# Float64 weights to float32: two ScalarE passes and one VectorE instruction per chunk in place of one and three

## The chip, the core and the metric

The kernel runs on one core of a Trainium2 chip. The metric is the device time of one execution in microseconds, taken as the median of three runs. Five engines work side by side, each through its own list of instructions in order: TensorE (PE: matmuls, with its weight loads listed as PEld), VectorE (DVE), ScalarE (ACT), GpSimd (POOL) and SyncE (SP), which here only issues DMA transfers. An instruction at the head of a list that waits for another engine or for a transfer holds up everything behind it in that list.

## What is computed

Eight batches of 576 tokens go through a two-step attention with 8 heads and 32 packed queries, then through a Fourier mixing, a normalisation and a two-layer network with residual:

```python
p_packed = sm_attn(p, k, v)              # p: 32 packed queries per head
out = sm_attn(q, p_packed, p_packed)
x = out.transpose(0, 2, 1, 3).reshape(B, S, H * D)
...
mixed = np.real(np.fft.fft(np.fft.fft(x, axis=1), axis=2)).astype(np.float32)
u = x + mixed
un = (u - mean(u)) / np.sqrt(var(u) + 1e-06)
ch = np.maximum(un @ w_ch1, 0.0) @ w_ch2
return (u + ch).astype(np.float32)
```

`w_ch1` (512 x 2048) and `w_ch2` (2048 x 512) arrive as float64; every other input is float32.

## The kernel before

**Tiles.** The 4608 token rows are worked in 9 tiles of 512 rows. `front(b)` computes attention and Fourier mixing of batch b, which fill the rows `u`; `ffn` runs the network on one tile. While `ffn` of tile t runs on PE, `front(t + 1)` is issued in small steps in between, so that the two share all engines. Before tile 0 stands only `front(0)`.

**The network.** The hidden dimension is cut into 16 blocks j (`NJ`). Per block, `up` (L637) makes 12 matmuls of 128x512 into a bank `ph`; ACT takes the relu of it, rounded to a matmul's precision, as `hh` (L643), DVE the remainder as `hl` (L644); then `down` (L654) makes 12 matmuls with the `hh` and `hl` of the block before into `acc`. So each block has one `hl`, and the 16 `hl` of a tile are a clock of its progress; I count them from hl 0. Each weight block is split likewise: `wr_h` by ACT (L99) and `wr_l` by POOL (L100).

**The weights.** There are 32 chunks of 128x512 numbers: `w1f[:, j]` and `w2f[:, j]` for each j. The float64 chunk is loaded as pairs of 32-bit words (low, high), 512 KB, into a staging place: the first six into parts of `w1f` and `w2f` that are still free, the others in turn into one place in `ubuf` and two buffers `wst`. `load_weights` (L167 to L170) turns it into float32 bits in place of the final chunk `c`: ACT takes the absolute value of the high word, read as a float32, times 2^-112 (which moves the exponent's bias); DVE shifts it left by 3, then ors in the three top bits of the low word, then the sign bit of the high word. The chunks are converted once, during `front(0)` and tile 0 (`LEAD` = 2 blocks ahead in the code); all other tiles find them in place.

**What sets the order.** From tile 1 on the order on PE, DVE, ACT and POOL is that of the code (`manual_schedule`, L738). Up to the end of tile 0 a scheduler of the framework orders each engine's list by its own estimate of the times, so a change in `load_weights` moves everything around it. The loads of keys (`kp`), values (`vt`) and queries (`qt`) for `front(1)` share one pool of two buffers (`ld`, L222) and stand in SP's list between the weight loads (L155). Such a load waits until the matmuls that read the buffer's last content are done; a weight load waits until DVE has finished with its staging place.

Of the kernel before, what the change touches and what calls it, by code (L numbers as in the profile page):

```python
# [9 lines left out]
F32 = mybir.dt.float32  # L10
F32R = mybir.dt.float32r
I32 = mybir.dt.int32
AF = mybir.ActivationFunctionType
ALU = mybir.AluOpType
AX = mybir.AxisListType
# [36 lines left out]
NE = 289  # L52
N2 = 258
REBIAS = 2.0 ** -112

# [20 lines left out]
def tile_kernel(ctx, tc, kpT, qT, v, w1, w2, tabs, tabR, tabB, tabT, sel, ident_d, out):  # L78
    nc = tc.nc
# [32 lines left out]

    nc.scalar.activation(small.tile([P, 1], F32, tag="ri", name="warm"), mhalf, AF.Exp)
    ubuf = cpool.tile([P, NU, DM], F32, name="ubuf")
# [26 lines left out]
    def spot(n, part, shape):  # L141

        t = (w1f, w2f)[n].rearrange("p j n -> p (j n)")[:, (part % NJ) * DM:]
        size = shape[1] * shape[2]
        return t[:, 0:size].rearrange("p (a n) -> p a n", a=shape[1])

    def fetch(j, n):
        i = stages.pop(0)
        if i is None:
            st = work.tile([P, 512, 2], I32, tag="wst", name="wst", bufs=2)  # L150
        elif i < 0:
            st = spot(n, i, [P, 512, 2]).bitcast(I32)
        else:
            st = ubuf[:, i:i + 2, :].rearrange("p a n -> p (a n)").bitcast(I32).rearrange("p (n t) -> p n t", t=2)
        nc.sync.dma_start(st, (w1, w2)[n][:, j, :].bitcast(I32).rearrange("p (n t) -> p n t", t=2))  # L155
        fetched[j, n] = st

    def load_weights(j):

        for n, dst in enumerate((w1f, w2f)):  # L160
            if (j, n) not in fetched:
                fetch(j, n)
            st = fetched.pop((j, n))
            low, high = st[:, :, 0], st[:, :, 1]
            c = dst[:, j, :].bitcast(I32)

            nc.scalar.activation(c.bitcast(F32), high.bitcast(F32), AF.Abs, scale=REBIAS)  # L167
            nc.vector.tensor_scalar(c, c, 3, None, ALU.logical_shift_left)
            nc.vector.scalar_tensor_tensor(c, low, 29, c, ALU.logical_shift_right, ALU.bitwise_or)  # L169
            nc.vector.scalar_tensor_tensor(c, high, -0x80000000, c,  # L170
                                           ALU.bitwise_and, ALU.bitwise_or)

# [26 lines left out]
    def statistics(key):  # L201
# [3 lines left out]
        def squares():  # L205
            junk = work.tile([P, DM], F32, tag="tmp", name="junk", bufs=3)
            nc.scalar.activation(junk, u, AF.Square, bias=st[:, 1:2], scale=-1.0, accum_out=st[:, 2:3])  # L207

# [22 lines left out]
    def front(b):  # L231
# [31 lines left out]
        def scores(*gs):  # L263
# [11 lines left out]
            for g in gs:  # L275
# [7 lines left out]
                for c, w in ((1, slice(512, S)), (0, slice(0, 512))):  # L283
                    nc.scalar.activation(e1[:, w], sc[g][c], AF.Exp,
                                         bias=nb, scale=0.125, accum_out=sm2[:, c:c + 1])
# [80 lines left out]
        def less_one(g):  # L366
# [6 lines left out]
            def exps():  # L373
                nc.scalar.activation(s2, s2, AF.Exp, scale=0.125)
                nc.scalar.activation(s2, s2, AF.Copy, bias=-1.0)

# [338 lines left out]
    for j in range(ORDER[0].count("D"), LEAD):  # L715
        load_weights(j)
# [3 lines left out]
    for t, (first, tk) in enumerate(tiles):  # L720

        gen = front(t + 1) if t + 1 < B else iter(())
        ended = []

        def step(i):

            next_step()
            if t > 0 and i in (0, 2):
                next(rest, None)
            elif not ended and next(gen, None) == "rest":  # L730
                ended.append(gen)
            if t == 0 and i % 2 == 0 and i // 2 + LEAD < NJ:
                load_weights(i // 2 + LEAD)
            assert i < 2 * NJ - 1 or t + 1 >= B or ended

        nxt = Turned(tiles[t + 1][1]) if t + 1 < len(tiles) else None

        with tc.manual_schedule(engines=MANUAL) if t > 0 else nullcontext():  # L738
            ffn(first, cur, step, nxt, t + 1 >= B)
        cur, rest = nxt, gen  # L740
# [112 lines left out]
```

## Time and profile before

| what | us |
|---|---|
| median of 3 runs (1038.54 to 1040.67) | 1039.46 |
| span of the profiled execution, first to last instruction | 1035.7 |
| the part of the median outside such a span | 3.8 |
| hl 0 of tile 0 starts at | 70.18 |
| hl 0 of tile 1 starts at | 201.82 |
| hl 0 of tile 2 starts at | 310.76 |

The page gives the profiled execution its span alone (its own device time is not listed), so I set the 3.8 us between span and median down as a constant. The first 70 us are `front(0)`; tile 0 takes 131.6 us from its hl 0 to the next tile's, tile 1 takes 108.9. In the views, busy times are per engine, "x" counts instructions, and the row of a wait gives the total, the number of times and the longest.

### The profile page before, as it was taken

The numbers are of one execution on the slowest core, as the hardware profiler recorded it, in microseconds if no ns is written. First come the engines' busy times: TensorE is split into PE (matmuls) and PEld (weight loads), VectorE is DVE, ScalarE is ACT, GpSimd is POOL, SyncE is SP. The second block draws the span as 40 slices with busy tenths as digits, with TensorE's granted clock in tenths as the row PEclk, the third lists the DMA queues.
The fourth block names the chain that finished last, engine by engine and source line by source line (L and its number), as shares of the span: only waits on it lengthen the run. The fifth ranks groups of instructions, "written<-read, shape, count | busy, mean of one in ns | idle before, by whom it ended". The sixth has DMA issues, their size and how long they took to land.

```text
span 1035.7 us, 14903 instructions
## 1 busy us (share of the span) xinstructions
PE 975.5 (94%) x5692; PEld 796.0 (77%) x5692; DVE 631.8 (61%) x1291; ACT 423.7 (41%) x878; POOL 472.2 (46%) x426
## 2 busy tenths in 40 slices
PE   4298789999999999999999999999999999999998
PEld 2276567878887888878877887788778888887886
DVE  4889999468565775578555946685658562114112
ACT  3445445334444444444354344444444443333322
POOL 3625545355344543454335434543345444444443
PEclk9599989999999999999999999999999999999999
DMA  9227424130003100310022002200120000001001
GB/s 359 96 67 231 132 63 122 63 123 1 1 23 118 47 1 1 138 49 1 1 95 92 1 1 92 95 1 1 47 92 0 2 11 31 0 1 41 1 1 41
DMA packets 18184, 59.10 MB, mean 57 GB/s; under 512 B 2166, under 2 KB 3008, under 8 KB 18112
## 3 DMA queue, kind: packets, MB, share of 16 engines
q1 hardware_dynamic: 17136, 56.70, 16.0%
q0 software_dynamic: 976, 1.44, 0.5%
q8 instruction: 45, 0.74, 0.3%
q14 instruction: 27, 0.22, 0.1%
HBM read 48.70 MB, written 9.44 MB: 56 GB/s over the span
## 4 chain that ended last, share of the span: by engine, by line
PE 75%; DVE 15%; ACT 4%; DMA 3%; issue 2%; POOL 1%; SPq 0%; ACTq 0%; DVEq 0%; POOLq 0%
PE ph L637 34%; PE acc L654 30%; DVE ubuf L557 2%; DVE turned L409 1%; DMA w2f<-w 1%; ACT hh L643 1%; DVE w2f L169 1%; ACT junk L207 1%; PE po L316 1%; DVE turned L405 1%; DMA w2f<-v 1%; DVE hl L644 1%; DVE w1f L169 1%; PE untp L598 1%; POOL wr_l L100 1%
## 5 line engine op out<-in xcount | busy, mean ns | idle before, releaser
L100 POOL TENSOR_TENSOR wr_l<-w1f,wr_h 128x512 fp32r<-128x512 f32 x144 | 191.0, 1326 | 397.5 <-ACT wr_h L99 397.3
L644 DVE SCALAR_TENSOR_TENSOR hl<-ph,hh 128x512 fp32r<-128x512 f32 x144 | 98.7, 686 | 300.8 <-ACT hh L643 300.5
L637 PE MATMUL ph<-uh,wr_h 128*128 128x512 f32 (+1 forms) x580 | 231.3, 399 | 12.4 <-DVE hl L644 10.4
L100 POOL TENSOR_TENSOR wr_l<-w2f,wr_h 128x512 fp32r<-128x512 f32 x144 | 193.7, 1345 | 96.2 <-ACT wr_h L99 89.2
L654 PE MATMUL acc<-wr_l,hh 128*128 128x512 f32 x576 | 227.7, 395 | 2.9 <-POOL wr_l L100 2.9
L637 PE MATMUL ph<-uh,wr_l 128*128 128x512 f32 (+1 forms) x580 | 228.7, 394 | 0.0
L637 PE MATMUL ph<-ul,wr_h 128*128 128x512 f32 (+1 forms) x580 | 228.5, 394 | 0.0
L654 PE MATMUL acc<-wr_h,hh 128*128 128x512 f32 x576 | 228.3, 396 | 0.1
L654 PE MATMUL acc<-wr_h,hl 128*128 128x512 f32 x576 | 226.3, 393 | 0.0
L643 ACT ACTIVATE hh<-ph 128x512 fp32r<-128x512 f32 x144 | 85.9, 596 | 282.9 <-PE ph L637 282.6
L637 PEld LDWEIGHTS ph<-uh,wr_h 128*128 128x128 f32 x580 | 109.5, 189 | 47.1 <-DVE hl L644 13.0
L654 PEld LDWEIGHTS acc<-wr_l,hh 128*128 128x128 f32 x576 | 108.5, 188 | 26.6 <-POOL wr_l L100 5.3
L637 PEld LDWEIGHTS ph<-uh,wr_l 128*128 128x128 f32 x580 | 109.6, 189 | 24.0
L654 PEld LDWEIGHTS acc<-wr_h,hh 128*128 128x128 f32 x576 | 108.6, 189 | 24.8 <-ACT hh L643 1.0
L637 PEld LDWEIGHTS ph<-ul,wr_h 128*128 128x128 f32 x580 | 109.8, 189 | 21.8
L654 PEld LDWEIGHTS acc<-wr_h,hl 128*128 128x128 f32 x576 | 108.4, 188 | 23.1
L99 ACT CAST wr_h<-w2f 128x512 fp32r<-128x512 f32 x144 | 89.4, 621 | 10.4 <-PE ph L637 8.8
L99 ACT CAST wr_h<-w1f 128x512 fp32r<-128x512 f32 x144 | 88.4, 614 | 10.4 <-PE ph L637 3.1
L207 ACT ACTIVATE junk<-ubuf,stat 128x512 f32<-128x512 f32 x36 | 25.8, 717 | 71.1 <-DVE stat L203 71.1
L227 PE MATMUL py<-gh,fh 128*128 128x258 f32 x64 | 19.6, 307 | 28.6 <-ACT fh L469 28.6
L598 PE MATMUL untp<-ident,un 128*128 128x128 f32 x144 | 38.2, 282 | 2.4 <-DVE stat L203 2.0
L227 PEld LDWEIGHTS py<-gh,fh 128*128 128x128 f32 x64 | 13.1, 204 | 30.1 <-ACT fh L469 29.6
(201 smaller groups left out, 1349.0 us busy)
## 6 DMA issues: line engine op xcount, KB each, us to landing
kp<-kpT SPq DMA_DIRECT2D x16, 608.0 KB, 4.9
out<-ubuf SPq DMA_DIRECT2D x36, 256.0 KB, 2.1
vt<-v SPq DMA_DIRECT2D x14, 640.0 KB, 4.9
wst<-w SPq DMA_DIRECT2D x17, 512.0 KB, 3.7
qt<-qT SPq DMA_DIRECT2D x14, 576.0 KB, 4.9
ubuf<-w SPq DMA_DIRECT2D x9, 512.0 KB, 3.7
w1f<-w SPq DMA_DIRECT2D x3, 512.0 KB, 13.5
w2f<-w SPq DMA_DIRECT2D x3, 512.0 KB, 12.5
```

Of the source, the lines that this page charges most:

```text
L99: nc.scalar.copy(hi, src)
L100: (lo_eng or nc.vector).tensor_tensor(lo, src, hi.bitcast(F32), ALU.subtract)
L169: nc.vector.scalar_tensor_tensor(c, low, 29, c, ALU.logical_shift_right, ALU.bitwise_or)
L207: nc.scalar.activation(junk, u, AF.Square, bias=st[:, 1:2], scale=-1.0, accum_out=st[:, 2:3])
L227: nc.tensor.matmul(o, lh, rh, start=first, stop=False)
L316: nc.tensor.matmul(po[h * NPK:(h + 1) * NPK, :D], e1T[g][:kk, c, h * NPK:(h + 1) * NPK], vt[:kk, c, h * D:(h + 1) * D], start=(c == 0), st ...
L557: nc.vector.scalar_tensor_tensor(u_of[key], qe, sign, pe, ALU.mult, ALU.add, accum_out=stat_of[key][:, 0:1])
L598: nc.tensor.transpose(tp[:, c * P:(c + 1) * P], un[:, c * P:(c + 1) * P], ident)
L637: nc.tensor.matmul(ph[:, t], l[:, c * P:(c + 1) * P], r[:, c, t], start=(k == 0), stop=(k == 11))
L643: nc.scalar.activation(hh[:, :T], ph[:, :T], AF.Relu)
L644: nc.vector.scalar_tensor_tensor(hl[:, :T], ph[:, :T], 0.0, hh[:, :T].bitcast(F32), ALU.max, ALU.subtract)
L654: nc.tensor.matmul(acc[i], l[:, w], r, start=(j == 0 and k == 0), stop=(j == NJ - 1 and k == 2))
```

## The change

Per chunk, ACT now makes two passes and DVE one instruction:

```diff
+U8 = mybir.dt.uint8
...
+SIGN = -2.0 ** 32
...
-            low, high = st[:, :, 0], st[:, :, 1]
+            high = st[:, :, 1]
+            fifth = st.rearrange("p n t -> p (n t)").bitcast(U8).rearrange("p (n t) -> p n t", t=8)[:, :, 3]
             c = dst[:, j, :].bitcast(I32)
 
-            nc.scalar.activation(c.bitcast(F32), high.bitcast(F32), AF.Abs, scale=REBIAS)
-            nc.vector.tensor_scalar(c, c, 3, None, ALU.logical_shift_left)
-            nc.vector.scalar_tensor_tensor(c, low, 29, c, ALU.logical_shift_right, ALU.bitwise_or)
-            nc.vector.scalar_tensor_tensor(c, high, -0x80000000, c,
-                                           ALU.bitwise_and, ALU.bitwise_or)
+            nc.scalar.activation(c.bitcast(F32), high.bitcast(F32), AF.Prelu, scale=REBIAS, alpha=SIGN)
+            nc.scalar.activation(high, fifth, AF.Copy, scale=1.0 / 32, bias=-31.0 / 64)
+            nc.vector.scalar_tensor_tensor(c, c, 3, high, ALU.logical_shift_left, ALU.bitwise_or)
```

The first pass is a parametric relu: a positive number is scaled by 2^-112 as before; a negative one is multiplied by -2^32 as well, which makes it positive and sets a bit of the exponent that the shift by 3 carries into the sign's place. The second pass reads one byte of each 8, the low word's top byte, divides by 32 with an offset that makes the rounding a floor, and writes the result, the three top bits, as an integer over the high word. DVE then shifts and ors in one instruction. The DVE instruction now reads the staging place only after both passes, and a second ACT pass stands in ACT's list for each chunk.

The scheduler's lists move. First ACT's list in tile 0 as it was, from behind hh 3 up to hh 4 (`w1f`, `w2f` are chunks, `wst` and `ubuf` staging places, `pph` and `bdh` are of front(1)):

```order
L167 ACTIVATE w2f<-wst 128x512
L167 ACTIVATE w1f<-wst 128x512
L99 CAST wr_h<-w1f 128x512
L344 CAST pph<-pptp 128x128
L167 ACTIVATE w2f<-ubuf 128x512
L99 CAST bdh<-bd 128x256
L99 CAST wr_h<-w2f 128x512
L643 ACTIVATE hh<-ph 128x512
```

The same place now, from behind hh 3 up to hh 4 (line numbers are those of the changed kernel: L170 and L171 are the two passes, L101 is the cast, L644 is hh):

```order
L170 ACTIVATE w2f<-ubuf 128x512
L171 ACTIVATE ubuf<-ubuf 128x512
L170 ACTIVATE w1f<-wst 128x512
L101 CAST wr_h<-w1f 128x512
L171 ACTIVATE wst<-wst 128x512
L345 CAST pph<-pptp 128x128
L170 ACTIVATE w2f<-wst 128x512
L171 ACTIVATE wst<-wst 128x512
L101 CAST bdh<-bd 128x256
L170 ACTIVATE w1f<-ubuf 128x512
L644 ACTIVATE hh<-ph 128x512
```

Four chunks stand ahead of this hh where three stood, each with one pass more. Over the whole list, 15 chunks have passed ACT ahead of hh 0 where 9 had, and all 32 ahead of hh 7 where 22 had.

Next DVE in tile 0, from hl 2 to hl 3 (`pp` is of front(1)), before:

```order
L644 SCALAR_TENSOR_TENSOR hl<-ph,hh 128x512
L321 TENSOR_SCALAR pp_864<-po,ri 128x128
L168 TENSOR_SCALAR w1f<-w1f 128x512
L169 SCALAR_TENSOR_TENSOR w1f<-wst,w1f 128x512
L168 TENSOR_SCALAR w2f<-w2f 128x512
L170 SCALAR_TENSOR_TENSOR w1f<-wst,w1f 128x512
L169 SCALAR_TENSOR_TENSOR w2f<-wst,w2f 128x512
L170 SCALAR_TENSOR_TENSOR w2f<-wst,w2f 128x512
L168 TENSOR_SCALAR w1f<-w1f 128x512
L169 SCALAR_TENSOR_TENSOR w1f<-ubuf,w1f 128x512
L170 SCALAR_TENSOR_TENSOR w1f<-ubuf,w1f 128x512
L644 SCALAR_TENSOR_TENSOR hl<-ph,hh 128x512
```

And now, from hl 2 to hl 3 (L172 is the one instruction that is left per chunk, L645 is hl):

```order
L645 SCALAR_TENSOR_TENSOR hl<-ph,hh 128x512
L322 TENSOR_SCALAR pp_856<-po,ri 128x128
L172 SCALAR_TENSOR_TENSOR w1f<-w1f,ubuf 128x512
L172 SCALAR_TENSOR_TENSOR w2f<-w2f,wst 128x512
L172 SCALAR_TENSOR_TENSOR w1f<-w1f,wst 128x512
L645 SCALAR_TENSOR_TENSOR hl<-ph,hh 128x512
```

Nine conversion instructions between two hl became three; again three chunks.

Last SP's list, from the first staged chunk to the loads of the values, as a piece before:

```order
L155 DMA ubuf<-w 128x1024
L155 DMA wst<-w 128x1024 x2
L223 DMA vt<-v 128x1280
L155 DMA ubuf<-w 128x1024
L223 DMA vt<-v 128x1280
L155 DMA wst<-w 128x1024 x2
```

and now:

```order
L157 DMA ubuf<-w 128x1024
L157 DMA wst<-w 128x1024 x2
L157 DMA ubuf<-w 128x1024
L157 DMA wst<-w 128x1024 x2
L157 DMA ubuf<-w 128x1024
L157 DMA wst<-w 128x1024 x2
L224 DMA vt<-v 128x1280
L157 DMA ubuf<-w 128x1024
L157 DMA wst<-w 128x1024
L224 DMA vt<-v 128x1280
```

Six more weight loads stand ahead of the first load of values, and two in place of one between the two.

## The prediction

> **What bounds the kernel now.** I began with the page: which engine is busy in which slice of 26 us.
>
> ```profile
> span 1035.7 us, 14903 instructions
> ...
> DVE  4889999468565775578555946685658562114112
> ```
>
> DVE's row reads 9 from the fourth to the seventh slice and falls to 4 in the eighth: from about 78 to 180 us, tile 0, it is full, and nowhere later. So I took the pace of tile 0 from the timeline of DVE, by the starts of hl, one per block:
>
> ```profile
> 70.18 0.69 DVE L644 SCALAR_TENSOR_TENSOR hl<-ph,hh 128x512 fp32r<-128x512 f32 x1 [0.22 <-ACT hh L643]
> 129.46 0.68 DVE L644 SCALAR_TENSOR_TENSOR hl<-ph,hh 128x512 fp32r<-128x512 f32 x1
> 201.82 0.69 DVE L644 SCALAR_TENSOR_TENSOR hl<-ph,hh 128x512 fp32r<-128x512 f32 x1 [1.89 <-ACT hh L643]
> 247.26 0.65 DVE L644 SCALAR_TENSOR_TENSOR hl<-ph,hh 128x512 fp32r<-128x512 f32 x1
> 310.76 0.69 DVE L644 SCALAR_TENSOR_TENSOR hl<-ph,hh 128x512 fp32r<-128x512 f32 x1 [1.26 <-ACT hh L643]
> ```
>
> The rows are hl 0 and hl 7 of tile 0, hl 0 and hl 7 of tile 1, hl 0 of tile 2. From hl 0 to hl 7 tile 0 takes 59.3 us where tile 1 takes 45.4; from hl 7 to the next hl 0 it takes 72.4 where tile 1 takes 63.5. Tile 1 does the same work without conversions, and the last work of its front besides. So tile 0 is 13.9 + 8.9 = 22.8 us over a tile that PE alone paces. The busy times by stretch agree:
>
> ```profile
> core 0: us, PE busy (x) PEld busy (x) DVE busy (x) ACT busy (x) POOL busy (x), PEclk, DMA share, GB/s
> 70.20:129.50 59.30, 50.04 (x308) 36.21 (x308) 57.66 (x91) 27.01 (x54) 31.34 (x23) 0.97 0.60 188
> 129.50:201.80 72.30, 65.72 (x315) 54.23 (x316) 57.86 (x124) 31.85 (x65) 32.43 (x27) 0.95 0.26 81
> 201.80:310.80 109.00, 108.19 (x663) 88.99 (x662) 71.86 (x153) 47.18 (x101) 50.13 (x43) 1.00 0.12 41
> ```
>
> In the first half of tile 0 DVE works 57.7 of 59.3 us, while PE idles 9.3 and ACT over half the time; in tile 1 PE is full at clock 1.00. PE's waits from 66 to 190 us name the holder:
>
> ```profile
> PE ph L637 <- DVE hl L644: 10.4, 6, 3.7
> PE py L227 <- ACT fh L469: 3.4, 1, 3.4
> ```
>
> It is hl, which DVE does late; and each gap costs clock behind it (0.97 and 0.95). From tile 1 on the lists are those of the code, unchanged, so **only the time up to 201.8 us can change.**
>
> **What is removed on DVE.** The conversions of the three lines (L168, L169, L170, two rows each: first and second half of tile 0):
>
> ```profile
> 70.20:129.50 59.30, 9.73 (x15) 0.97 0.60 188
> 129.50:181.00 51.50, 4.35 (x11) 0.93 0.32 93
> ...
> 70.20:129.50 59.30, 16.51 (x15) 0.97 0.60 188
> 129.50:181.00 51.50, 8.02 (x11) 0.93 0.32 93
> ...
> 70.20:129.50 59.30, 11.01 (x14) 0.97 0.60 188
> 129.50:181.00 51.50, 12.09 (x12) 0.93 0.32 93
> ```
>
> That is 37.3 us in the first half and 24.5 in the second; without them 20.4 and 33.4 of other DVE work stay. By the new order 15 chunks are done ahead of hl 0, the other 17 between hl 0 and hl 7, none later. What one instruction costs, from the answers on lines L169 and L167 (min/median/max in ns):
>
> ```profile
> L169 DVE SCALAR_TENSOR_TENSOR w1f<-wst,w1f x8: 676/838/1672, 77.9 to 169.2; 128x512 int32<-128x512 int32 x8
> L167 ACT ACTIVATE w2f<-wst x9: 659/672/677, 34.1 to 174.7; 128x512 f32<-128x512 f32 x9
> ```
>
> The new DVE instruction has L169's form and operands, so 0.68 to 1.67 us each; I take 0.84, the median: 17 x 0.84 = 14.3 us (11.6 to 28). DVE then has 34.7 us of work in the first half, and is no longer the bound.
>
> The spread has a known shape. The Trainium skill (SBUF — State Buffer, section "Who interferes with whom") says that a DVE instruction with two SBUF inputs contends with a GpSimd instruction that reads SBUF, the later one blocked to the other's end, and that ACT never waits for anyone. The trace agrees: L169 reaches 1672 ns, ACT's pass stays within 659 to 677. By that rule the instruction that is kept is of the kind that still waits, and the sum would take 28 us for the 17 if each met one; it would leave DVE under 50 us, below the half.
>
> **What is added on ACT.** In the first half ACT's conversions take:
>
> ```profile
> 70.20:129.50 59.30, 8.86 (x14) 0.97 0.60 188
> ```
>
> Its other work there is 27.0 - 8.9 = 18.2 us. After: 17 chunks x 2 passes x 0.67 = 22.8 us, so 41 us in all; it fits. The trace has no parametric relu, no pass that reads single bytes 8 apart, and none that writes 32-bit words 8 bytes apart. Its read counterpart, the 8-byte-strided L167, is the nearest row (0.67); the upper end is 1.67, the worst L169. I take 0.67, the row that it is nearest to. Faster passes would gain nothing further, since ACT isn't the bound.
>
> **What paces the first half then: PE or the supply of chunks.** PE alone needs tile 1's 45.4 us. The supply is this: SP's waits up to 182 us, and the stretch without transfers ahead of tile 0:
>
> ```profile
> SPq L155 <- DVE w1f L170: 58.3, 12, 15.2
> SPq L223 <- PE s L259: 44.6, 2, 44.0
> SPq L155 <- DVE w2f L170: 30.1, 11, 5.1
> ...
> 40.00:70.00 30.00, 23.30 (x160) 21.20 (x160) 24.18 (x61) 14.48 (x33) 10.94 (x26) 0.75 0.00 1
> ```
>
> SP stood 44 us behind the first load of values, which waits for the score matmuls of front(1); all weight loads waited behind it, and 88 us went by waiting for DVE to free staging places. In the new list six more weight loads come ahead of that load, into those empty 30 us. What is left for the first half, by the list of transfers (KB each, us to landing) and the rate from 70 to 110 us:
>
> ```profile
> kp<-kpT SPq DMA_DIRECT2D x16, 608.0 KB, 4.9
> vt<-v SPq DMA_DIRECT2D x14, 640.0 KB, 4.9
> wst<-w SPq DMA_DIRECT2D x17, 512.0 KB, 3.7
> qt<-qT SPq DMA_DIRECT2D x14, 576.0 KB, 4.9
> ...
> 70.00:110.00 40.00, 36.58 (x246) 26.83 (x242) 38.18 (x62) 19.54 (x41) 20.35 (x15) 0.96 0.71 223
> ```
>
> 17 weight chunks, 2 vt, 2 qt and 1 kp are 12.0 MB. At 223 GB/s that is 54 us; but DMA was only 0.71 busy then, and 0.71 of 54, 38 us, is the other end. With three staging places a turn is 3.7 (landing) + 1.3 (two passes) + 0.84 + about 1.5 in queues = 7.3 us, so 17 chunks take 17 x 7.3 / 3 = 41 us, plus the five other loads in the same queue, 3.0 MB, 13 us at that rate if nothing overlaps. **I take 50.8 us for hl 0 to hl 7**, between 46.5 (PE) and 55 (supply), nearer to the middle than to either: a gain of 8.5 us (4.3 to 12.8).
>
> **The second half.** No chunk is left for it; 33.4 us of DVE work stand in some 65. The bound is PE's 63.5 us, a gain of 8.9. Of the waits, the 3.4 us for fh stay possible, since they end a chain of small DVE, POOL and ACT steps on the weights of front(1), which the scheduler has moved together. I take 66.9 us, **a gain of 5.5** (1 to 9).
>
> **The start of tile 0.** Ahead of hl 0 DVE does 15 conversion instructions for 19 shorter and longer ones: about even. ACT does 30 passes there for 9; three chunks' passes now stand between the last spectra and the last uh cast, which lets PE start:
>
> ```profile
> 65.72 0.58 ACT L99 CAST uh<-untp 128x512 fp32r<-128x512 f32 x1 [1.02 <-PE untp L598]
> ```
>
> The cover is ACT's idle time (it was idle over half of 40 to 70 us: 14.5 of 30 busy). Without it the cost is six passes, 4 us; with all of it and a freer DVE, -1. I take a **loss of 0.5**.
>
> **Sum:** -8.5 - 5.5 + 0.5 = -13.5 us on the span of 1035.7, so 1022.2; with the 3.8 us between span and median, 1026.0.
>
> **Rivals.**
> 1. *PE paces all of tile 0.* Chunks come early enough and the chain of front(1) keeps up: 12.8 + 8.9 - 0.5 = 21.2, so 1018.3. For it: 30 us of empty DMA time are put to use. Against it: 54 us of transfers at the rate seen.
> 2. *The supply stays the bound.* hl 7 stays near 129, the second half alone gains: 5.5 - 0.5, so 1034.5. For it: ACT already waits for chunks (below).
> 3. *A loop through the lists, and slower.* A chunk's load waits for DVE's instruction behind one hl, and its first pass stands ahead of the next hh but one or the next:
>
> ```profile
> ACT w2f L167 <- DMA wst<-w: 9.4, 6, 3.7
> ...
> L643 ACT ACTIVATE hh<-ph 128x512 fp32r<-128x512 f32 x144 | 85.9, 596 | 282.9 <-PE ph L637 282.6
> ```
>
> Here are ACT's wait for such loads and hh's duration (596 ns). A wait that used to cost ACT only idle time would then hold hh, hl, and through hl the next load. One turn is hl 0.69 + the instruction 0.84 + landing 3.7 + pass 0.67 + hh 0.60: 6.5 us; with both passes of two further chunks, 4 x 0.67, and a landing of 4.9 as for values, it is 10.4. It decides from 8.5 us a block on (59.3 / 7). At 10.4 in all seven: 73 us, 13.5 lost, 0.5 at the start, 5.5 regained: 1048. Against it: in the new list only hh 2 and hh 4 stand behind a chunk whose load follows the hl just before; the others have a block more.
> 4. *ACT's passes are dear.* At 1.3 us each ACT needs 18.2 + 44 = 62 us in the first half and becomes its bound: 3 to 5 us lost there, 5.5 regained: about 1039.
> 5. *The change brings more than it says: table loads.*
>
> ```profile
> 0.73 1.28 ACT L113 ACT_TABLE_LOAD   x1 [0.73 <-PEq L845]
> ```
>
> If the parametric relu didn't share a table with exp, each turn between the two in ACT's list (8) would cost such a load: 10 us at 1.28, all of it if on the path, so 1036. The new list still has one such load in all. The Trainium skill (ScalarE: Activation LUTs, section "Table sets: the hidden batching unit") names relu and abs, not this function, as members of exp's set, and puts a switch at about 2.7 us; by it the time would be some 21 us longer, about 1047. No run here shows a second load.
>
> **How the numbers follow.** Chances: forecast (1021 to 1031.5) 0.57, rival 1 0.14, rival 2 0.15, rival 3 0.07, rival 4 0.04, rival 5 0.03. The range runs from 1017 to 1035, which takes in the forecast and the first two rivals; the three bad ends of the sum at once (4.3, 1 and a late start by 4) would give 1038, the three good ones 1017. This kernel's measurement tells 0.2%, 2 us, from no change: faster (under 1037.4) is the forecast, rivals 1 and 2 and part of the others, 0.87; within it 0.04; slower 0.09.
>
> **What would show it.** DVE's row falls to 5 or 6 in the slices from 78 to 180 us; hl 7 of tile 0 starts near 121 and hl 0 of tile 1 near 188; PE's wait for hl falls under 4 us; weight transfers appear between 45 and 65 us; the ACT passes read 0.67. I am wrong if ACT waits for transfers right ahead of hh (rivals 2 and 3), if a pass is over 1 us, or if tile 0 starts later than 74.

## The result, and the profile after

The changed kernel takes 1030.86 us (median of 4 runs, 1030.17 to 1032.36) where the kernel before takes 1039.0 (4 runs, 1038.34 to 1040.67): a ratio of 0.9923, 95% interval 0.9909 to 0.9937. A later group of runs had 1031.69 (5 runs) against 1038.32 (13 runs), 0.9942 (0.9929 to 0.9955). So it is **faster by 6.6 to 8.1 us**, or 0.6 to 0.8%, where 13.5 us were forecast.

The page of the changed kernel: the span, the row of DVE in 40 slices of 26 us, and that of the DMA engines.

```profile
span 1028.4 us, 14863 instructions
...
DVE  4885963558465856577556846594658562114112
DMA  9358400220023000310041002200210000001001
```

The fourth to seventh slices of DVE, 9999 before, read 5963: DVE has room in part of tile 0, but from 103 to 128 us it still reads 9. The starts of hl 0 and hl 7 of tile 0 and of hl 0 of tiles 1 and 2, from the timeline of DVE:

```profile
73.06 0.68 DVE L645 SCALAR_TENSOR_TENSOR hl<-ph,hh 128x512 fp32r<-128x512 f32 x1
124.55 0.68 DVE L645 SCALAR_TENSOR_TENSOR hl<-ph,hh 128x512 fp32r<-128x512 f32 x1
193.86 0.69 DVE L645 SCALAR_TENSOR_TENSOR hl<-ph,hh 128x512 fp32r<-128x512 f32 x1 [1.89 <-ACT hh L644]
302.79 0.69 DVE L645 SCALAR_TENSOR_TENSOR hl<-ph,hh 128x512 fp32r<-128x512 f32 x1 [1.27 <-ACT hh L644]
```

| stretch | before | changed | difference | forecast |
|---|---|---|---|---|
| start to hl 0 | 70.18 | 73.06 | +2.88 | +0.5 |
| hl 0 to hl 7 | 59.28 | 51.49 | -7.79 | -8.5 |
| hl 7 to hl 0 of tile 1 | 72.36 | 69.31 | -3.05 | -5.5 |
| tile 1 | 108.94 | 108.93 | 0 | 0 |

Tile 2 starts 8.0 us earlier, and the spans differ by 7.3; the 0.7 us between them stand behind that point, where the lists are the same.

The busy times of the two halves of tile 0 and of a stretch that lies across them, in the columns of the table of windows shown in the prediction:

```profile
73.00:124.50 51.50, 46.55 (x302) 34.78 (x298) 37.53 (x60) 37.97 (x70) 27.03 (x21) 1.00 0.71 230
124.50:193.90 69.40, 63.53 (x316) 53.41 (x317) 37.83 (x93) 26.57 (x56) 30.68 (x28) 0.95 0.04 16
...
103.00:136.00 33.00, 23.52 (x113) 17.39 (x111) 32.10 (x53) 20.01 (x37) 21.02 (x19) 0.96 0.34 108
```

DVE works 37.5 of 51.5 us in the first half, 57.7 of 59.3 before, and ACT 38.0 against 27.0. Weight transfers now end with the first half (DMA share 0.04 in the second, 0.26 before). But PE still idles 5 us in the first half and 6 in the second, which has a clock of 0.95. Of these 10.8 us, 9.5 lie between 103 and 136 us, and there DVE works 32.1 of 33 us, nearly as much as before (33.0). So DVE was relieved in the first 30 us of tile 0 and at its end, not in between. The waits of PE from 60 to 190 us, and those of SP up to 182:

```profile
PE ph L638 <- DVE hl L645: 9.4, 4, 5.1
...
SPq L157 <- DVE w1f L172: 31.2, 7, 17.0
SPq L157 <- DVE w2f L172: 20.6, 8, 4.7
SPq L224 <- PE s L260: 10.7, 2, 9.4
```

SP's wait for the score matmuls fell from 44.6 to 10.7 us, and the one of 3.4 us for fh is gone from PE's list. The wait for hl stands at 9.4 us: fewer times (4 for 6), but one of 5.1. The timeline of PE there, with the wait for hl 7 and the one for hl 8, and then the longest pieces of the chain of waits ahead of it:

```profile
125.29 0.50 PE L638 MATMUL ph<-uh,wr_h 128*128 128x512 f32 x1 [2.65 <-DVE hl L645]
125.62 0.39 PE L638 MATMUL ph<-ul,wr_h 128*128 128x512 f32 x1
...
136.11 0.79 PE L638 MATMUL ph<-uh,wr_h 128*128 128x512 f32 x1 [5.09 <-DVE hl L645]
136.70 0.63 PE L638 MATMUL ph<-ul,wr_h 128*128 128x512 f32 x1
```

```profile
125.23 1.00 DVE d L385
126.25 1.23 DVE z L386
...
130.80 1.85 DVE f L446 x6
132.65 1.15 DVE f L454
...
135.46 0.61 DVE hl L645
```

These ten microseconds of DVE, from `d` to `eo`, are front(1)'s attention weights (`d` to `a`, 5.5 us) and its fold (`f` to `eo`, 4.7 us), put ahead of hl 8 in DVE's list. The wait costs 5.09 us, and ten matmuls behind it take 0.57 to 0.79 us apiece in place of 0.39.

Not all of the ten are DVE's own work. `d` and `z` are instructions of 128x18 that take 1.07 and 1.23 us here and 0.16 us each in the kernel before (at 129.05 and 130.06). POOL works on two `wr_l` at that time, and `d` and `z` end 0.04 and 0.03 us behind them; the copy `f` of L454 ends 0.02 us behind a third. By these rows some 3 us of the ten are waits for POOL (an estimate: 0.9 and 1.1 for `d` and `z`, and 1.1 for a copy that takes 0.15 us in the run pin below).

### The profile page after: what moved, and what is told of

It reads as the page before. It is cut to its first block, busy times and chain, and to the rows that moved or that the text cites. A ratio compares the mean times of both kernels' runs of the same rounds, so it can differ in the third digit from the quotient of the medians.

```text
span 1028.4 us, 14863 instructions
## 1 busy us (share of the span) xinstructions
PE 970.6 (94%) x5692; PEld 791.5 (77%) x5692; DVE 595.7 (58%) x1227; ACT 441.7 (43%) x910; POOL 469.8 (46%) x426
## 4 chain that ended last, share of the span: by engine, by line
PE 78%; DVE 11%; ACT 5%; issue 2%; POOL 2%; DMA 1%; ACTq 0%; DVEq 0%; POOLq 0%
PE ph L638 35%; PE acc L655 31%; DVE turned L410 2%; DVE ubuf L558 1%; ACT hh L644 1%; DVE turned L406 1%; PE po L317 1%; PE s L260 1%; DMA ubuf<-w 1%; ACT junk L208 1%; POOL wr_l L102 1%; DVE hl L645 1%; PE py L228 1%; PE py L229 1%; PE py L230 1%
## 5 line engine op out<-in xcount | busy, mean ns | idle before, releaser
L645 DVE SCALAR_TENSOR_TENSOR hl<-ph,hh 128x512 fp32r<-128x512 f32 x144 | 98.9, 687 | 310.7 <-ACT hh L644 310.5
L644 ACT ACTIVATE hh<-ph 128x512 fp32r<-128x512 f32 x144 | 85.9, 597 | 282.4 <-PE ph L638 282.3
L101 ACT CAST wr_h<-w1f 128x512 fp32r<-128x512 f32 x144 | 88.3, 613 | 14.5 <-PE acc L655 8.1
L101 ACT CAST wr_h<-w2f 128x512 fp32r<-128x512 f32 x144 | 89.4, 621 | 8.4 <-PE ph L638 6.7
L228 PE MATMUL py<-gh,fh 128*128 128x258 f32 x64 | 18.7, 294 | 27.4 <-ACT fh L470 27.4
L102 POOL TENSOR_TENSOR gl<-turned,gh 128x516 fp32r<-128x516 f32 x16 | 25.4, 1587 | 21.9 <-ACT gh L101 21.9
```

The costliest lines, as they stand in the source:

```text
L101: nc.scalar.copy(hi, src)
L102: (lo_eng or nc.vector).tensor_tensor(lo, src, hi.bitcast(F32), ALU.subtract)
L228: nc.tensor.matmul(o, lh, rh, start=first, stop=False)
L644: nc.scalar.activation(hh[:, :T], ph[:, :T], AF.Relu)
L645: nc.vector.scalar_tensor_tensor(hl[:, :T], ph[:, :T], 0.0, hh[:, :T].bitcast(F32), ALU.max, ALU.subtract)
```

## Experiments

All twelve are timed against the kernel before on the same chip; the runs of one group share a chip and the runs of before, whose median was 1040.32, 1038.90 and 1038.32 us in the three groups. The changed kernel ran in group 3 and for the result above; its two ratios differ by 2 us, so a difference of that size between groups tells nothing.

| group | run | us, median (range) | ratio to before (95%) |
|---|---|---|---|
| 1 | vt_spot | 1036.09 (1034.04 to 1037.35) | 0.9956 (0.9940 to 0.9972) |
| 1 | sign_only | 1029.47 (1028.85 to 1030.94) | 0.9889 (0.9871 to 0.9908) |
| 1 | byte_only | 1030.82 (1029.63 to 1032.21) | 0.9905 (0.9886 to 0.9923) |
| 1 | act3 | 1030.86 (1029.11 to 1031.16) | 0.9901 (0.9884 to 0.9918) |
| 2 | pin | 1030.12 (1028.80 to 1030.37) | 0.9911 (0.9889 to 0.9933) |
| 2 | late | 1029.39 (1029.17 to 1031.22) | 0.9911 (0.9892 to 0.9930) |
| 2 | both | 1026.98 (1026.53 to 1027.50) | 0.9884 (0.9867 to 0.9901) |
| 2 | sign_vt | 1031.60 (1030.25 to 1033.26) | 0.9929 (0.9909 to 0.9949) |
| 3 | change_again | 1031.69 (1030.74 to 1033.96) | 0.9942 (0.9929 to 0.9955) |
| 3 | dve3 | 1040.30 (1037.22 to 1042.65) | 1.0022 (1.0009 to 1.0035) |
| 3 | both_again | 1028.02 (1027.14 to 1030.38) | 0.9906 (0.9890 to 0.9921) |
| 3 | sign_both | 1028.82 (1028.58 to 1029.86) | 0.9914 (0.9900 to 0.9927) |

**Was it DVE's work or the early loads?** Two things changed at once: DVE lost two of three instructions per chunk, and six more weight loads went into the empty stretch ahead of tile 0. The first run, on the kernel before, was meant to give the loads alone:

```diff
-            vts[g] = load(v[b, :, g], [P, 5, 4 * D], "vt", (g, 4) if b == 0 else None)
+            vts[g] = load(v[b, :, g], [P, 5, 4 * D], "vt", (g, (4, 13)[b]) if b < 2 else None)
```

> The kernel before with one edit: the values of front(1) are loaded into a place of their own (parts of w1f and w2f that are free until chunk 13) and not into the shared pool of two, so the weight loads behind them in SP's list need not wait for front(1)'s score matmuls. The conversions stay one ACT pass and three DVE instructions. Theory A (the gain came from DVE's load in tile 0): DVE still does about 62 us of conversions in tile 0, so the time stays within 2 us of before: 1037 to 1041. Theory B (the gain came from weight loads that land in the 30 us without transfers ahead of tile 0): SP's wait of 44 us goes and most of the 8 us are gained without any change of the conversions: 1031 to 1034.

It gained 4.2 us, between the two. SP's list was not freed as wholly as meant:

```profile
SPq L223 <- DVE w1f L170: 26.4, 1, 26.4
SPq L223 <- PE s L259: 16.4, 2, 15.9
```

The place of the values had a chunk in it still, so SP stood 26 us there, and then 15.9 us at the first load of queries. The values did come early (50.19 and 56.19 us), but the next weight load started at 75.58 us, where before it was 73.32. So this run moves the values and leaves the weights where they were; early weight loads alone are not tested by it. In the profiled execution, the slowest of the five, tile 0 takes 129.0 us (72.43 to 201.41) against 131.6; where the rest of the 4.2 lies isn't shown.

The half of the change that keeps the three low bits on DVE, one ACT pass and two DVE instructions:

```diff
             nc.scalar.activation(c.bitcast(F32), high.bitcast(F32), AF.Prelu, scale=REBIAS, alpha=SIGN)
-            nc.scalar.activation(high, fifth, AF.Copy, scale=1.0 / 32, bias=-31.0 / 64)
-            nc.vector.scalar_tensor_tensor(c, c, 3, high, ALU.logical_shift_left, ALU.bitwise_or)
+            nc.vector.tensor_scalar(c, c, 3, None, ALU.logical_shift_left)
+            nc.vector.scalar_tensor_tensor(c, low, 29, c, ALU.logical_shift_right, ALU.bitwise_or)
```

> The changed kernel with half of the change: the parametric relu puts the sign in place, but the three low bits come by DVE again (shift, then or): one ACT pass and two DVE instructions per chunk. 10 chunks have passed ACT ahead of hh 0 (before 9, changed 15). Theory A (DVE's load): two instructions of 0.65 and 1.0 us for some 22 chunks are about 36 us of DVE in tile 0, against 62 before and 15 changed; a little over half of the 8 us: 1033 to 1036. Theory B (chunks that come ahead of tile 0): with 10 chunks ahead against 9 the time stays near before: 1037 to 1039.

And the other half, the byte by ACT and the sign by DVE:

```diff
-            nc.scalar.activation(c.bitcast(F32), high.bitcast(F32), AF.Prelu, scale=REBIAS, alpha=SIGN)
-            nc.scalar.activation(high, fifth, AF.Copy, scale=1.0 / 32, bias=-31.0 / 64)
-            nc.vector.scalar_tensor_tensor(c, c, 3, high, ALU.logical_shift_left, ALU.bitwise_or)
+            nc.scalar.activation(c.bitcast(F32), high.bitcast(F32), AF.Abs, scale=REBIAS)
+            nc.scalar.activation(low, fifth, AF.Copy, scale=1.0 / 32, bias=-31.0 / 64)
+            nc.vector.scalar_tensor_tensor(c, c, 3, low, ALU.logical_shift_left, ALU.bitwise_or)
+            nc.vector.scalar_tensor_tensor(c, high, -0x80000000, c,
+                                           ALU.bitwise_and, ALU.bitwise_or)
```

> The other half of the change: ACT takes the absolute value and, in a second pass, the byte with the three low bits; DVE shifts and ors in one instruction and ors the sign in another: two ACT passes and two DVE instructions per chunk, both with two SBUF inputs. Theory A: as in the other half, but each DVE instruction has two SBUF inputs (0.84 us and up, some over 1.6 beside POOL): 1034 to 1037. Theory B: 10 chunks ahead of hh 0, so 1037 to 1039. If ACT's second pass costs by itself, this half stands over the other by as much as it costs.

Both were faster than either theory had it: 1029.5 and 1030.8, as low as the whole change. **One DVE instruction less per chunk brings the whole gain; of the second no gain can be measured.** And it does so almost without the early loads: sign_only starts one weight load at 59.43 and one at 70.20 us, byte_only one at 66.77, where the changed kernel has started six by 60 us. (The scheduler orders its lists anew in both halves, so what one instruction less brings includes what was moved with it: with these loads ahead of the first load of values, SP's wait for the score matmuls is 2.2 us in sign_only, for 44.6 before.) The windows from 40 to 70 us and the two halves of tile 0 of sign_only:

```profile
40.00:70.00 30.00, 21.12 (x140) 18.97 (x141) 24.54 (x65) 13.42 (x32) 11.53 (x31) 0.76 0.05 19
...
72.70:125.40 52.70, 47.42 (x302) 34.72 (x301) 43.76 (x79) 28.52 (x56) 28.26 (x22) 0.97 0.70 240
125.40:195.20 69.80, 64.73 (x322) 53.85 (x321) 44.08 (x104) 29.88 (x62) 29.98 (x28) 0.98 0.14 48
```

The DMA share ahead of tile 0 is 0.05, next to the changed kernel's 0.34 and the 0.00 of before; yet the halves take 52.7 and 69.8 us, within 1.2 of the changed kernel's. DVE works 6 us more in each of them, and in the profiles this costs 1.7 us of tile 0 (122.5 for 120.8; byte_only has 123.1), which the medians don't show. But DVE is not free for that: its row reads 6993 in the fourth to seventh slices, and from 103 to 136 us it works 32.3 of 33 us, as in the changed kernel. PE idles 15.8 us in tile 0 before, 10.8 in the changed kernel and 10.4 here, and of the last two 9.5 and 8.6 lie in that stretch. It is full with one instruction per chunk as with two; why the second doesn't shorten it isn't shown. This is also where theory A, as I had written it, was wrong too: it counted the gain in proportion to the work taken away.

Both at once, the half change and the place for the values (the edits are those of sign_only and vt_spot):

> The half of the change with one ACT pass and two DVE instructions (which ran at 0.9889 of before), with the values of front(1) in a place of their own besides (which alone ran at 0.9956). If the two act on different limits (DVE's work; chunks that arrive late), the gains add: about 0.984 to 0.986 of before. If the first already lets enough chunks through ahead of tile 0 (11 against 9 of before), nothing is added: 0.987 to 0.991.

0.9929, where sign_only had 0.9889: nothing is added, and the figure lies above both of the expected ranges. The first weight loads stand as in sign_only (58.53 and 69.30 us), so here too only the values were moved; whether that costs time can't be told between two groups.

**DVE's work put back** into the changed kernel:

```diff
             nc.vector.scalar_tensor_tensor(c, c, 3, high, ALU.logical_shift_left, ALU.bitwise_or)
+            nc.vector.tensor_scalar(c, c, 0, None, ALU.logical_shift_left)
+            nc.vector.scalar_tensor_tensor(c, c, 0, c, ALU.logical_shift_left, ALU.bitwise_or)
```

> The changed kernel with DVE's work of before put back: behind each DVE instruction of a chunk stand two more that leave it as it is (a shift by 0, and an or of the chunk with itself). ACT's passes, the loads and the splits are the changed kernel's. Theory A (DVE's third instruction per chunk is what was paid): 32 x 1.4 to 2 us of DVE come back, some 25 to 35 us of them in tile 0, and at least 5 of the 8 us are lost: 1035 to 1041. Theory B (what was gained is the loads' place in the lists, ahead of tile 0, which stays): 1030 to 1033.

All of the gain is lost, and 2 us more. Its page, and its windows (40 to 70 us, then the two halves of tile 0):

```profile
DVE  4799999358665775568465937685658662114112
...
40.00:70.00 30.00, 22.00 (x137) 20.59 (x138) 24.15 (x58) 14.49 (x33) 11.68 (x25) 0.71 0.00 1
...
71.70:128.60 56.90, 50.43 (x312) 36.23 (x308) 55.53 (x90) 35.21 (x68) 30.89 (x23) 0.97 0.60 196
128.60:205.20 76.60, 67.05 (x315) 54.76 (x316) 59.39 (x127) 37.56 (x76) 33.30 (x28) 0.93 0.24 76
```

DVE's row is full again. But the run is less clean than its expectation says: the loads did not stay where they were (share 0.00 from 40 to 70 us), since the scheduler's own estimate counts DVE's time too and moved the chunks back (9 through ACT ahead of hh 0, as before; 15 in the changed kernel). It shows that ACT's passes bring nothing by themselves; that the six early loads aren't needed is shown by sign_only and byte_only. Six early loads beside a full DVE are in no run, so what they would bring alone stays open.

**What ACT's passes cost.** A third pass per chunk:

```diff
             nc.scalar.activation(c.bitcast(F32), high.bitcast(F32), AF.Prelu, scale=REBIAS, alpha=SIGN)
+            nc.scalar.activation(c.bitcast(F32), high.bitcast(F32), AF.Prelu, scale=REBIAS, alpha=SIGN)
```

> The changed kernel with the parametric relu pass issued twice per chunk (the second writes the same words again): three ACT passes, one DVE instruction. Theory A (ACT has idle time that covers its passes): 32 x 0.67 = 21 us more of ACT move the time by 0 to 2 us: 1030 to 1033. Rival (ACT's passes stand between the spectra and tile 0's start, and between hh and hl, and are paid): a third to a half of the 21 us: 1037 to 1042. In either case hl 0 shows by how much the start is later than 73.1 us.

0.9901: no cost that can be measured. hl 0 is at 75.04 us, 0.8 to 2.0 later than in the two profiles of the changed kernel (73.06 and, below, 74.22), and tile 0 takes 119.4 us (to 194.45) in place of 120.8, so most of the late start is regained.

**The two places where the forecast was short.** First the fold, the second part of what stands ahead of hl 8 (`i` counts front(1)'s steps, `t` the tile):

```diff
-            nc.vector.scalar_tensor_tensor(hl[:, :T], ph[:, :T], 0.0, hh[:, :T].bitcast(F32), ALU.max, ALU.subtract)
+            last_hl[0] = nc.vector.scalar_tensor_tensor(hl[:, :T], ph[:, :T], 0.0, hh[:, :T].bitcast(F32),
+                                                        ALU.max, ALU.subtract).ins
...
-            elif not ended and next(gen, None) == "rest":
-                ended.append(gen)
+            elif not ended:
+                with tc.issue_after(last_hl[0]) if t == 0 and i >= 16 else nullcontext():
+                    if next(gen, None) == "rest":
+                        ended.append(gen)
```

> The changed kernel with front(1)'s steps from the 16th on in tile 0 queued behind the block's hl, so that hl 8 no longer stands on DVE behind 10 us of front(1)'s fold work (in the changed kernel hl 7 starts at 124.55 and hl 8 at 135.38, with a PE wait of 5.09 us for it, and 12 matmuls behind the gap take 5.03 us and not 2.75). Theory A (the second half gained 3 and not 5.5 us because of this order): hl 8 starts by 131, the wait and part of the clock behind it go: 4 to 6 us less, 1025 to 1027. Rival (the fold work is on the path of front(1) anyway, so that a later wait of PE for fh, fl or the spectra takes its place): within 1.5 us of the changed kernel, 1029.5 to 1032.

The order did what it should, and in the time the rival held. The rows of hl 8 and of the next hl of DVE, and PE's waits behind them:

```profile
132.05 0.69 DVE L646 SCALAR_TENSOR_TENSOR hl<-ph,hh 128x512 fp32r<-128x512 f32 x1
...
138.76 0.69 DVE L646 SCALAR_TENSOR_TENSOR hl<-ph,hh 128x512 fp32r<-128x512 f32 x1
```

```profile
137.77 0.39 PE L229 MATMUL py<-gh,fh 128*128 128x258 f32 x1 [1.95 <-ACT fh L471]
138.77 0.58 PE L231 MATMUL py<-gh,fl 128*128 128x258 f32 x1 [0.49 <-DVE fl L477]
```

hl 8 comes 6.2 us behind hl 7 (10.8 before this edit), and the wait of 5.09 us is gone. But the next matmuls in PE's list are front(1)'s, which need that very fold: fh and fl are now waited for, and hl 10 comes 25.7 us behind hl 7 where it came 27.4, so of the 4.6 us won at hl 8 there are 1.8 left. The second half takes 68.0 us, not 69.3, and the time stays within 1.5 us of the changed kernel.

Second, the start. POOL's first three wr_l were put ahead of front(0)'s fold in the changed kernel; here they and the ACT casts that feed them stand behind its last instruction, `fold_end`:

```diff
-                split(hi, lo, (w1f, w2f)[n][:, j, :], nc.gpsimd)
+                with tc.issue_after(fold_end[0]) if nsplit[0] < 3 else nullcontext():
+                    split(hi, lo, (w1f, w2f)[n][:, j, :], nc.gpsimd)
+                nsplit[0] += 1
```

> The changed kernel with POOL's first three wr_l queued behind the last fold instruction of front(0); in the changed kernel they stand ahead of it, and DVE's fold chain of front(0) runs 2.3 to 3.5 us later than before. Theory A (tile 0 starts 2.9 us later because POOL's wr_l hold POOL and stretch DVE's instructions beside them): hl 0 starts at 70.5 to 71.5 and the time is 1.5 to 2.5 us less: 1028.5 to 1029.5. Rival (the start is late because DVE and ACT do six more chunks ahead of it, or because these wr_l are needed by the first block at once): hl 0 at 72.5 or later, 1030 to 1033.

hl 0 started at 72.82, only 0.24 us earlier. The fold's last steps and what follows, on DVE and POOL in this run, then on DVE in the changed kernel:

```profile
47.12 1.29 DVE L480 TENSOR_TENSOR fl<-f,fh 128x776 fp32r<-128x776 f32 x1 [1.29 <-ACT fh L474]
48.33 1.79 DVE L174 SCALAR_TENSOR_TENSOR w2f<-w2f,wst 128x512 int32<-128x512 int32 x1
50.04 1.78 DVE L174 SCALAR_TENSOR_TENSOR w1f<-w1f,wst 128x512 int32<-128x512 int32 x1
51.75 0.75 DVE L104 TENSOR_TENSOR yl<-py,yh 128x258 fp32r<-128x258 f32 x2
```

```profile
46.29 3.27 POOL L104 TENSOR_TENSOR wr_l<-w1f,wr_h 128x512 fp32r<-128x512 f32 x2
49.53 1.75 POOL L104 TENSOR_TENSOR wr_l<-w2f,wr_h 128x512 fp32r<-128x512 f32 x1
```

```profile
49.68 0.97 DVE L476 TENSOR_TENSOR fl<-f,fh 128x776 fp32r<-128x776 f32 x1 [1.29 <-ACT fh L470]
50.56 0.68 DVE L172 SCALAR_TENSOR_TENSOR w2f<-w2f,wst 128x512 int32<-128x512 int32 x1
51.16 0.68 DVE L172 SCALAR_TENSOR_TENSOR w1f<-w1f,wst 128x512 int32<-128x512 int32 x1
51.77 0.75 DVE L102 TENSOR_TENSOR yl<-py,yh 128x258 fp32r<-128x258 f32 x2
```

The fold is 2.6 us earlier, as theory A says. Then the moved wr_l meet the next two conversions: 1.79 and 1.78 us beside POOL, 0.68 each without. yl starts at 51.75 against 51.77, and the gain is gone. The collision was moved, not removed. The time of this run, 1029.39, lies in theory A's range all the same and within 1.5 us of the changed kernel, so it decides nothing.

Both edits together:

> The two orders of the runs before it together. If both theories A hold, the gains add: 1023 to 1025.5. If only the order of hl 8 counts: 1025 to 1027. If neither: 1029.5 to 1032.

1026.98, then again, with more rounds and beside the changed kernel itself:

> The changed kernel with both orders (POOL's first splits behind front(0)'s fold, front(1)'s fold behind the block's hl), again with more rounds: if the gain over the changed kernel is real, 3 to 5 us under it in this call; if it was chance, within 1.5 us of it.

1028.02 (1027.14 to 1030.38) against 1031.69 (1030.74 to 1033.96) in the same group: 3.7 us less, with no overlap of the runs. It is **faster than both kernels**, by 10.3 us than before. Where the 3.7 us lie is only partly seen: its first profile has tile 0 at 118.0 us (73.39 to 191.38), its second at 120.4 (73.20 to 193.63), the changed kernel's at 120.8 and 121.0. Nor is it shown why the two edits bring more together than the 0.7 and 1.5 us that each alone lies under the result. And the same orders on the half change:

> One ACT pass and two DVE instructions per chunk (the half of the change that keeps the three low bits on DVE), with both orders. If the two orders act alike on this half: 2 to 5 us under the changed kernel, as the one before it. If DVE's second instruction now stands in the way, it is 1 to 4 us over the one before it.

1028.82: the same as with the whole change, so DVE's second instruction is not in the way here either. That the orders help the half change is not shown by it: sign_only had 0.9889 without them, in its own group.

The last run was the changed kernel again, for the spread of its start:

> The changed kernel again, beside the three others of this call on one chip: 0.990 to 0.994 of before. Of its profile: by chance alone the start of tile 0 (hl 0, 73.06 us in the first profile) should differ, since the kernel with the values in a place of their own, whose lists equal those of before up to hl 2, started it 2.25 us later than before (72.43 against 70.18); 72 to 75.5 here if so, within 0.3 us of 73.06 if not.

hl 0 started at 74.22, 1.16 us later than in its first profile. In these two profiles tile 0 took 120.80 and 120.96 us: its pace repeats, its start does not. The same shows in vt_spot, whose lists are those of before up to hl 2. One instruction of front(0), in the timeline of DVE of before and then of vt_spot:

```profile
23.51 0.74 DVE L371 TENSOR_TENSOR s<-s,m 128x576 f32<-128x576 f32 x1
```

```profile
24.68 1.86 DVE L371 TENSOR_TENSOR s<-s,m 128x576 f32<-128x576 f32 x1
```

And POOL's instruction at that time, again before and then vt_spot:

```profile
24.67 1.41 POOL L100 TENSOR_TENSOR gl<-turned,gh 128x516 fp32r<-128x516 f32 x1 [5.95 <-ACT gh L99]
```

```profile
24.65 1.28 POOL L100 TENSOR_TENSOR gl<-turned,gh 128x516 fp32r<-128x516 f32 x1 [5.64 <-ACT gh L99]
```

Before, DVE's instruction was over at 24.25, ahead of POOL's. In vt_spot it came 0.03 us behind POOL's start and took 1.1 us more; DVE's list was 1.2 us late there already, for a reason that isn't shown. Hit or missed by a fraction of a microsecond, such a meeting moves what stands behind it.

## Why the prediction was right or wrong

**What bounded the kernel: right in kind.** DVE's conversions held tile 0. Taking one instruction per chunk away gives the whole gain, and putting two back takes it all (with the chunks moved back as well, as told above).

**The durations: right for ACT, short for DVE.** The new ACT passes and the DVE instruction, by line (min/median/max in ns):

```profile
L170 ACT ACTIVATE w2f<-wst x9: 657/676/691, 35.5 to 120.1; 128x512 f32<-128x512 f32 x9
L171 ACT ACTIVATE wst<-wst x17: 633/675/699, 45.3 to 122.6; 128x512 int32<-128x512 uint8 x17
L172 DVE SCALAR_TENSOR_TENSOR w2f<-w2f,wst x9: 681/693/1797, 50.6 to 123.3; 128x512 int32<-128x512 int32 x9
L115 ACT ACT_TABLE_LOAD x1 | 1.3, 1283 | 0.7 <-PEq L846 0.7
```

Both passes take the 0.67 us that I took from L167, so rival 4 is out. There is one table load, so rival 5 is out, in the form that the Trainium skill gave it too (ScalarE: Activation LUTs, section "Table sets: the hidden batching unit"): the function that it doesn't name costs no switch here. The DVE instruction's median is 0.69 us, where I took 0.84, but the longest takes 1.80, past my upper end of 1.67, and the 17 in the first half take 16.5 us and not 14.3. With them DVE had 37.5 us of work there where I had 34.7.

**The first half: the size right (7.8 for 8.5), the reason half right.** I set 50.8 us between PE's pace and the supply of chunks, and hl 0 to hl 7 took 51.5. Up to 100 us the chain of waits does contain transfers:

```profile
79.59 3.59 DMA ubuf<-w
93.17 5.86 DMA ubuf<-w
```

From there to hl 7 it holds none, only DVE's and ACT's steps of front(1), hh and hl, with the conversions between them. In the last 21.5 us ahead of hl 7 DVE works 20.8: "no longer the bound" held for the first 30 us of this half and not for the rest. So it is in part luck that the size came out. The lower end of 46.5 us has no row behind it either; tile 1's half, from which it came, takes 45.4. And the whole second DVE instruction could stay without a loss, which my account of DVE's hours didn't see.

**The second half: the step that failed.** "No chunk is left for it; 33.4 us of DVE work stand in some 65. The bound is PE's 63.5 us, a gain of 8.9." The first part held, and DVE's work was 37.8 us of 69.4, but I read a mean load as freedom. Ten of these microseconds stand in one piece ahead of hl 8, and PE waits 5.09 us there, with a slower clock behind; some 3 of the ten are DVE's waits for POOL, which the sum had nothing for. The gain was 3.05 us, not 5.5. I had kept a wait for fh in the sum and none for hl; the runs show that these are one and the same work: ahead of hl the fold delays hl (the changed kernel), behind it the fold delays fh (pin). The second half takes 69.3 us the one way and 68.0 the other, not PE's 63.5. Nor does "each gap" cost clock: in the kernel before, the wait of 2.27 us ahead of 120.79 is followed by matmuls of 0.39 and 0.40 us, the usual time.

**The start: mis-sized in this pair of profiles, +2.9 for +0.5, and part of it chance.** "The cover is ACT's idle time" was the step to doubt: the mean over 40 to 70 us hid that in its last part ACT has none. From 55.8 to 67.4 us, the changed kernel:

```profile
55.80:67.40 11.60, 10.09 (x74) 7.80 (x72) 11.29 (x35) 11.16 (x25) 2.43 (x4) 1.00 0.43 136
```

ACT (the fourth of the busy times) works 11.2 of 11.6 us, nine conversion passes among them; before it worked 6.4. Still, hh 0 is only 1.2 us later (70.77 for 69.56); the rest of the 2.9 stands on DVE, where a conversion of 1.78 us went ahead of hl 0. By hl 1 the delay is 1.0 us (77.83 for 76.80). How much belongs to the change can't be said from these profiles: with the lists of before hl 0 was seen at 70.18 and 72.43, with those of the changed kernel at 73.06 and 74.22.

**The time around the span: wrong in what it was.** I added 3.8 us as a constant. Every run after gives both: 1030.17 us had a span of 1028.4, 1.8 less. With that 1.8, the profiled execution of before took about 1037.5 us (an estimate), and the other 2 us are by how much it was quicker than its median; its hl 0 at 70.18 us, against 72.43 with the same lists in vt_spot, fits that. So the pair of profiles (7.3 us apart) shows too large a loss at the start and too small a gain in all.

**The rivals.** PE does not pace all of tile 0 (rival 1). The supply did not stay the bound (2): hl 7 came at 124.55, not 129. The loop (3) did not bound: ACT's waits for transfers fell (those for `wst` from 16.7 us to 3.8, two groups each). Its first link is there, though, and I had named it as a sign of being wrong: the hh at 83.80 and 99.61 stand right behind a pass that had waited 0.82 and 1.02 us for a transfer. PE waited 0.20 us behind the second and not at all behind the first.

**The signs.** Weight transfers ahead of tile 0 and passes of 0.67 us came as said. DVE's row kept a 9, PE's wait for hl stands at 9.4 us where it was to fall under 4, which both point at the stretch from 103 to 136 us, as the second half does. Tile 1 starts at 193.86, not near 188, and tile 0 at 73.06 in the first profile and 74.22 in the second, past the 74 that I had set as a sign of being wrong.

## What to carry to other kernels

When an engine is full in one stage, take from it only until the next limit shows: here one of the two instructions brought all of the gain, and one run for each half of a change tells it. A mean load over a stage says nothing about the instruction that others wait for (DVE was busy 73% of the first half here, and 97% of its last 21.5 us); look at what stands ahead of that instruction in its engine's list, and before moving that aside, ask who needs the moved work next. And a single profile's start can be off by 2 us, so lay the pace of a stage beside it in two executions.

## What the runs showed of the hardware

DVE instructions with two inputs in SBUF took 1.1 us more beside a POOL instruction in these rows: 0.68 and 1.79 us for one conversion, 0.74 and 1.86 for `s<-s,m`. The Trainium skill has the rule (SBUF — State Buffer, section "Who interferes with whom"): the later one of the two is blocked to the other's end. These rows agree with it: the two conversions of the run late end 0.56 and 0.54 us behind the POOL instruction beside them, and `s<-s,m` 0.61, about what each takes alone. Instructions with one input were held as well: `d` and `z` of 128x18, 1.07 and 1.23 us for 0.16. What I hadn't expected is its reach: one such meeting is 1.1 of the 2.25 us by which two executions with the same lists up to there differ at the start of tile 0.

A PE wait of 5.09 us is followed by ten matmuls of 0.57 to 0.79 us, and one of 2.65 us (ahead of 125.29) by matmuls of 0.39 us from the second on, the usual time. The 12 matmuls of the block took 4.87 us (136.11 to 140.98) against 2.85 (125.29 to 128.14), so the price there was 2 us on top of the wait; the granted clock from 136 to 145 us was 0.75. But the length of the wait alone doesn't decide it. In the second profile of the changed kernel the wait for hl 7 is 2.67 us, and eight matmuls of 0.54 to 0.63 us follow from 127.66 on:

```profile
126.81 0.50 PE L638 MATMUL ph<-uh,wr_h 128*128 128x512 f32 x1 [2.67 <-DVE hl L645]
...
127.66 0.63 PE L638 MATMUL ph<-uh,wr_h 128*128 128x512 f32 x1
```

In sign_vt a wait of 3.81 us (ahead of 137.49) is followed by matmuls of 0.39 and 0.40 us. What decides isn't shown here.

An ACT pass that reads single bytes 8 apart and writes 32-bit integers 8 bytes apart takes 0.675 us, as long as the first pass, which stays in float32 (0.676).
